# Two decode layers in one core: a ring of three places instead of four, one more key part kept on the chip, and the end of the second up matrix loaded in another shape

## The chip, the cores and the metric

The kernel runs on one core of a Trainium2 chip. The metric is device time in microseconds (us) for one execution of the whole program; each kernel is timed in several runs on the same chip, and the median is given. A profile of one execution of the program gives the detail: its busy times per engine (PE does matrix products, DVE, ACT and POOL elementwise work, SP only issues loads), its waits, and what the sixteen DMA engines moved.

## What is computed

Two layers, with the same weights and caches in both, each made of an attention block and a gated MLP, for one new token of a batch of two:

```python
def _A_ref(x, k_cache, v_cache, wq, wo):
    # B=2, Sq=1, D=576, H=32, Dh=128, Sk=8192
    q = (x @ wq).reshape(B, Sq, H, Dh).transpose(0, 2, 1, 3)
    scores = jnp.einsum("bhqd,bhkd->bhqk", q, k_cache) * (Dh ** -0.5)
    p = softmax(scores)
    o = jnp.einsum("bhqk,bhkd->bhqd", p, v_cache)
    return o.transpose(0, 2, 1, 3).reshape(B, Sq, H * Dh) @ wo

def _B_ref(x, w_gate, w_up, w_down):   # Df = 4608
    return (gelu(x @ w_gate) * (x @ w_up)) @ w_down

x = x + _A_ref(layernorm(x), k_cache, v_cache, wq, wo)
x = x + _B_ref(layernorm(x), w_gate, w_up, w_down)
x = x + _A_ref(layernorm(x), k_cache, v_cache, wq, wo)
x = x + _B_ref(layernorm(x), w_gate, w_up, w_down)
```

All of it is in float32. The two caches hold 268 MB each, and each layer reads both.

## The kernel before

**Items and parts.** The caches are cut into items: 30 items of two heads of one batch entry each (`PAIRS`), and four of a single head (`SINGLE`). An item's keys or values come in parts of 128 partitions by 16 rows of 128 numbers, `PART` = 2048 floats per partition, 1024 KB. A pair item has 8 parts, a single one has 4. The first layer walks through the items from first to last, the second from last to first, so that what the first layer read last can stay on the chip. The keys of the last two single items (62 and 63 in the names below) and the values of the last three stay whole. Of the item `SINGLE[1]`, which is third in the second layer, one key part of four stays: the first layer copies part 3 into a PSUM tile, `kept` (line 636), and the second copies it back into the place of part 0 (line 679).

**The arena.** All that is loaded goes into one tile, `space`, of `END` floats per partition. An `Arena` keeps track of what is live. Six slots of four parts each begin at 0; pairs of slots hold pair items. Between the layers the last slot's room, from `RING` on, is used as a ring of `NPLACE` places of `PLACE` = 2304 floats (9216 bytes per partition, 1152 KB for a whole place). In the second layer's MLP no ring is used: `fit` looks for the first free stretch in all of `space`.

**The queue of loads.** `plan_first`, `plan_mlp` and `plan_second` append every load, in order, to one list. `pump` issues loads from the head of the list for as long as there is room, and stops at the first one that has none; each time a reader is done with a piece (`done`), `pump` goes on. All loads are issued by SP, in this order. When the program runs, an issue waits until the last reader of the bytes it overwrites has finished, and everything behind it waits too. There are eight landing semaphores, taken in turn, so an issue also waits for the landing of the load eight before it.

**What goes through the ring.** In order: the eight pieces of `wo` in the first layer (`out_rows`, line 296); 18 pieces of the first MLP's gate and up (`split_rows` and `split_middle`, lines 248 and 258), each read as two or four loads; nine of the down matrix (`down`, lines 271 and 275); nine pieces of wq for the second layer (`of_half` and `half_rows`, lines 238 and 227); then three key parts of `SINGLE[1]` and one of `SINGLE[0]` (`one`, line 165). Before that, two places hold the products of the kept keys (`products`): the keys must not be overwritten, so the products of items 62 and 63 go there.

**Attention.** For each item, DVE multiplies the key parts by the query (line 644), POOL adds the two halves of the 128 products (line 661) and DVE sums the rest (line 664); ACT takes the exponentials (line 721); PE multiplies the weights with the values (line 762). For the first items of the second layer some of the work is moved to POOL and ACT. At the end PE multiplies with `wo` (line 812).

**The MLP.** After a layer norm (`norm`), `xt` holds the transposed input in nine blocks of 32 columns, one for each of the nine rows that a partition holds of the matrix halves. In the second layer `all_products` multiplies gate and then up: each of the nine half rows `u` of a partition has eight sixteenths of `HG` = 288 columns, and each is one matrix product (line 967). The list `GU` says how many half rows one load carries: three and three and three for gate, three, three, one, one, one for up. Then `activate` makes `hT`, and the down products follow (line 1004). `idle_products` (line 526) are products whose result nobody reads.

## Time and profile before

| | |
|---|---|
| time, median of 3 runs | 2686.63 us (2686.57 to 2686.77) |
| the profiled execution | 2686.79 us, span 2685.0 us |
| read from HBM | 1153.18 MB, 429 GB/s over the span |
| busy: PE, DVE, POOL, ACT | 914.4, 1806.0, 1161.8, 163.7 us |
| mean granted PE clock | 0.642 |
| the chain that ended last, by share | DMA 28%, DVE 13%, POOL 3% |

In the views, L644 is line 644 of the kernel. A row of the timeline gives the start and the length in us, the engine, the line, the operation and the tiles, the number of instructions merged, and in brackets the idle time of the engine before it and what ended it. A row of the windows gives the stretch, its length, the busy time of PE, weight loads, DVE, ACT and POOL with the number of instructions, the granted PE clock, the DMA engines' mean busy share (it can read slightly over 1, since packets overlap a little) and GB/s. A row of waits gives who waited for whom, the sum, the count, and the longest. Matrix products in float32 appear as two passes each, so a count such as x16 stands for eight products.

### The profile page before, as it was taken

The page shows a single profiled execution, that of the slowest core. Times are in us where ns is not written, and L with a number is a line of the kernel's source. Part 1 is how long each engine was busy: PE and PEld are TensorE (multiplying, and loading weights), DVE is VectorE, ACT ScalarE, POOL GpSimd, SP SyncE. Part 2 cuts the span into 40 slices and gives each one's busy share as a digit, 9 for nine tenths or more (in the row PEclk, how much of TensorE's full clock was granted, in tenths as well). Part 3 has the DMA queues.
Part 4 walks back from the last instruction along what each step waited for, and adds up shares of the span by engine and source line. Part 5 has one row for each costly group of instructions (what it writes and reads, how often), then busy time and mean ns, then how long its engine had stood idle before and what let it go on. Part 6 is the DMA issues. An engine that isn't in the chain of part 4 may idle for free. (4 is left out here: it accounts for less than half of the span.)

```text
span 2685.0 us, 17174 instructions
## 1 busy us (share of the span) xinstructions
PE 914.4 (34%) x7150; PEld 305.4 (11%) x7150; DVE 1806.0 (67%) x874; ACT 163.7 (6%) x786; POOL 1161.8 (43%) x261
## 2 busy tenths in 40 slices
PE   1323332332233233334663333233223323332356
PEld 0100010010001000111221101001000100010022
DVE  4876687677667766867037877667766776776640
ACT  0000000000000000000026000000000000000000
POOL 2543454354445444544028455445444543454420
PEclk7656666665666566566986665666566656656678
DMA  9999999999999999999999999999999999999998
GB/s 422 436 436 426 437 432 434 433 434 432 433 431 435 436 428 433 436 428 425 414 418 434 431 431 436 431 434 434 437 428 434 434 435 431 431 434 435 433 421 375
DMA packets 33950, 1154.30 MB, mean 430 GB/s; under 512 B 4152, under 2 KB 4176, under 8 KB 5968
## 3 DMA queue, kind: packets, MB, share of 16 engines
q1 hardware_dynamic: 33832, 1153.19, 99.8%
q8 instruction: 56, 0.92, 0.1%
q14 instruction: 22, 0.18, 0.0%
q10 hardware_dynamic: 40, 0.01, 0.0%
HBM read 1153.18 MB, written 0.00 MB: 429 GB/s over the span
## 5 line engine op out<-in xcount | busy, mean ns | idle before, releaser
L661 POOL TENSOR_TENSOR space<-space 128x3072 f32<-128x3072 f32 (+3 forms) x221 | 1128.6, 5107 | 1263.3 <-DVE space L644 1202.5
L644 DVE TENSOR_TENSOR space<-space,bank 128x6144 f32<-128x6144 f32 (+3 forms) x223 | 1112.7, 4991 | 560.2 <-DMA space<-in_A_k_cache_dram 496.8
L762 PE MATMUL acc<-space,prz 128*8 128x512 f32 x4096 | 594.6, 744 | 199.4 <-DMA space<-in_A_v_cache_dram 195.5
L664 DVE TENSOR_REDUCE S<-space 128x48 f32<-128x3072 f32 (+3 forms) x223 | 569.3, 2553 | 89.9 <-POOL space L661 89.6
L592 PE MATMUL bank<-qsb,pick 4*64 4x128 f32 (+1 forms) x256 | 46.3, 436 | 863.1 <-DVE space L644 853.1
L762 PEld LDWEIGHTS acc<-space,prz 128*8 128x8 f32 x4096 | 119.1, 104 | 616.3 <-issue 410.6
L784 PE MATMUL bank<-of,osb 128*32 128x2 f32 x512 | 40.9, 202 | 324.4 <-DVE osb L777 324.4
L713 ACT ACTIVATE nbs<-bank 128x2 f32<-128x2 f32 (+1 forms) x68 | 11.6, 171 | 1848.2 <-PE bank L698 1801.8
L592 PEld LDWEIGHTS bank<-qsb,pick 4*64 4x64 f32 (+1 forms) x256 | 20.7, 202 | 882.5 <-DVE space L644 863.2
L517 POOL TENSOR_TENSOR rstd<-ve,mhalf 128x1 f32<-128x1 f32 x4 | 2.2, 550 | 168.8 <-DVE ve L515 168.8
L690 PE MATMUL bank<-ident,m 128*1 128x128 f32 x68 | 19.5, 286 | 160.7 <-DVE m L688 160.5
L784 PEld LDWEIGHTS bank<-of,osb 128*32 128x32 f32 x512 | 35.9, 154 | 331.7 <-DVE osb L777 330.5
L978 DVE STREAM_TRANSPOSE o<-o 128x288 f32<-128x288 f32 x4 | 2.8, 691 | 94.5 <-ACT o L976 94.5
L729 PE MATMUL bank<-sums,unit 128*128 128x2 f32 x120 | 35.2, 363 | 87.0 <-ACT prz L721 87.0
L776 DVE TENSOR_TENSOR acc<-acc,diag 128x512 f32<-128x512 f32 x64 | 43.5, 680 | 22.0 <-PE acc L762 22.0
L721 ACT ACTIVATE prz<-S,nbs 64x128 f32<-64x128 f32 (+1 forms) x128 | 50.7, 396 | 17.3 <-POOL prz L711 14.4
L803 ACT ACTIVATE oT<-bank,rinv 32x8 f32<-32x8 f32 x110 | 28.5, 259 | 381.5 <-PE bank L784 380.8
L654 ACT ACTIVATE space<-space 128x128 f32<-128x128 f32 x164 | 48.3, 296 | 23.6 <-DVE space L644 21.7
L698 PE MATMUL bank<-m,unit 1*128 1x2 f32 (+1 forms) x136 | 39.0, 354 | 25.3 <-DVE m L696 25.3
L777 DVE TENSOR_REDUCE osb<-acc 128x128 f32<-128x512 f32 x64 | 44.3, 691 | 2.2
L521 DVE TENSOR_TENSOR x<-bank,x 128x144 f32<-128x144 f32 x4 | 1.2, 308 | 64.1 <-PE bank L1004 40.4
L729 PEld LDWEIGHTS bank<-sums,unit 128*128 128x128 f32 x120 | 30.1, 311 | 92.2 <-ACT prz L721 92.2
(73 smaller groups left out, 427.6 us busy)
## 6 DMA issues: line engine op xcount, KB each, us to landing
space<-in_A_v_cache_dram SPq DMA_DIRECT2D x8, 4096.0 KB
space<-in_A_k_cache_dram SPq DMA_DIRECT2D x6, 4096.0 KB
space<-in_A_wo_dram SPq DMA_DIRECT2D x15, 1152.0 KB
space<-in_A_k_cache_dram SPq DMA_DIRECT2D x15, 1024.0 KB
space<-in_B_w_down_dram SPq DMA_DIRECT2D x9, 1152.0 KB
space<-in_B_w_gate_dram SPq DMA_DIRECT2D x3, 3456.0 KB
space<-in_A_v_cache_dram SPq DMA_DIRECT2D x10, 1024.0 KB
space<-in_A_wq_dram SPq DMA_DIRECT2D x3, 3072.0 KB
```

What stands on the lines that cost most here:

```text
L592: nc.tensor.matmul(qb[n][to, :], pick[32 * c:32 * c + 4, r:r + 1].to_broadcast([4, P // it.heads]), qsb[32 * c:32 * c + 4, (h % 4) * DH:(h ...
L644: nc.vector.tensor_tensor(out=u[:, :rows, :], in0=t[:, :rows, :], in1=qb[n].unsqueeze(1).to_broadcast([P, rows, DH]), op=ALU.mult)
L654: nc.scalar.activation(u[:, j, :], u[:, j, :], AF.Copy, accum_out=S[n][:, k * JC + j:k * JC + j + 1])
L661: nc.gpsimd.tensor_tensor(out=half, in0=half, in1=u[:, :r, DH // 2:], op=ALU.add)
L664: nc.vector.tensor_reduce(out=S[n][:, k * JC:k * JC + own_rows(n, k, m)], in_=prod.pop((n, k)), axis=AX.X, op=ALU.add)
L698: nc.tensor.matmul(mT[n][:, :heads], ones[0:1, :], m1[:, :heads], start=True, stop=True)
L721: nc.scalar.activation(pr[at, lo:].rearrange("p (g e) -> p g e", e=4)[:, 0:it.rows // 2:2, :], s[at, :it.rows].rearrange("p (g r) -> p g r ...
L729: nc.tensor.matmul(tot[n][:, :ITEMS[n].heads], ones, rs.pop(n), start=True, stop=True)
L762: nc.tensor.matmul(accumulator(n)[32 * c:32 * c + 8, :], pr[:, at:at + 8], t[g // 4][:, g % 4 * 4:g % 4 * 4 + 4, :].rearrange("p j d -> p ...
L776: nc.vector.tensor_tensor(out=q, in0=q, in1=diag.unsqueeze(2).to_broadcast([P, 4, DH]), op=ALU.mult)
L777: nc.vector.tensor_reduce(out=t, in_=q.rearrange("p r d -> p d r"), axis=AX.X, op=ALU.add)
L784: nc.tensor.matmul(po[lo:lo + 32, i, :], t[:, i::GH], of, start=True, stop=True)
```

## The change

The ring has three places instead of four. The room behind it, `STAY`, holds part 2 of the keys of `SINGLE[1]` from the first layer to the second; part 3 stays in PSUM as before. Both copies are made by ACT when the first part of that item is multiplied in the first layer. The second layer reads two parts of that item instead of three. `END` shrinks by 256 floats. The products of the kept keys go to places 1 and 2 instead of 2 and 3.

In the second MLP, the up matrix's half rows 6 to 8 are one load of 128 partitions without the last two sixteenths of half row 8 (`upper_rows`). These two sixteenths, `LOWER` = 2, are loaded for all 128 rows onto partitions 0 to 63 (`lower_rows`): those of rows 0 to 63 and, beside them, those of rows 64 to 127. They come in eight loads of 8 partitions each (every fourth partition of 32), four before and four after the last gate load. PE takes them last, in four products over 64 partitions, for which `norm` adds a transpose of the upper 64 partitions' last block to the lower ones. Two small tiles change their place or grow by 32 columns.

```diff
--- before.py
+++ after.py
@@ -32,15 +32,17 @@
 PAD = 6
 NT = 4
 NI = DF // (NT * P)
+LOWER = 2
 CW = D // 4
 
 PART = JC * DH
 SLOT = 4 * PART
 NSLOT = 6
 PLACE = DF // 2
-NPLACE = 4
+NPLACE = 3
 RING = 5 * SLOT
-END = RING + NPLACE * PLACE
+STAY = RING + NPLACE * PLACE
+END = STAY + PART
 HELD = 5
 
 
@@ -239,6 +241,32 @@
 
         weights(("wq", 1, h, k), width, None, transfers)
 
+    def upper_rows(key, w, us, first, lower):
+
+        n = len(us) * w.shape[1] // 2 - lower * HG
+        rows = w.rearrange("r (s w) -> (r s) w", s=2).rearrange("(p u) w -> p (u w)", p=P)
+        lo = us[0] * w.shape[1] // 2
+        weights(key, n, first, lambda t: nc.sync.dma_start(t, rows[:, lo:lo + n]))
+
+    def lower_rows(key, w, first, lower):
+
+        width = w.shape[1] // 2
+        rows = w.rearrange("r (s w) -> (r s) w", w=width).rearrange("(e p u) w -> p e u w", e=2, u=NU)
+        rows = rows[:, :, NU - 1, width - lower * HG:]
+        weights(key, 2 * lower * HG, first, lambda t: None)
+
+        def eighth(at):
+            def make():
+                nc.sync.dma_start(ready[key][at], rows[at])
+                return True
+
+            return lambda: queue.append(make)
+
+        return [eighth(slice(lo + j, lo + 32, 4)) for lo in range(0, HALF, 32) for j in range(4)]
+
     def split_rows(name, w, h, u):
 
         rows = w[:, DF // 2 * h:DF // 2 * (h + 1)].rearrange("(m r) w -> m r w", r=NU)
@@ -279,7 +307,7 @@
     def products():
 
         def make():
-            at = [RING + k * PLACE for k in (2, 3)]
+            at = [RING + k * PLACE for k in (1, 2)]
             if not all(arena.clear(a, PLACE) for a in at):
                 return False
             ready["products"] = [part(arena.take(("products", k), at[k], PART)) for k in range(2)]
@@ -302,7 +330,7 @@
 
     single = [range(u, u + 1) for u in range(NU)]
     three = [range(u, u + 3) for u in range(0, NU, 3)]
-    GU = [three, three[:-1] + single[-3:]]
+    GU = [three, three]
 
     DOWN = [
         [[(t, i) for i in range(lo, lo + 4)] for t in range(NT) for lo in (0, 4)] + [[(t, NI - 1) for t in range(NT)]],
@@ -369,7 +397,7 @@
         last = PAIRS - 1
         k63, v63, k62, v62 = ("k", 1, SINGLE[3]), ("v", 1, SINGLE[3]), ("k", 1, SINGLE[2]), ("v", 1, SINGLE[2])
 
-        for k in range(3):
+        for k in range(2):
             one(("k", 1, SINGLE[1]), kc, SINGLE[1], k, None)
         for k in range(4):
             one(("k", 1, SINGLE[0]), kc, SINGLE[0], k, (k63, k - 1) if k else None)
@@ -405,9 +433,17 @@
                 for u in range(4):
                     split_rows("u", wu, h, u)
         else:
-            for g, (name, w) in enumerate((("g", wg), ("u", wu))):
-                for us in GU[g]:
-                    half_rows((name, layer, us[0]), w, us, 0)
+            for i, us in enumerate(GU[0]):
+                if i == 2:
+                    short = lower_rows(("u", layer, NU), wu, 0, LOWER)
+                    for make in short[:4]:
+                        make()
+                half_rows(("g", layer, us[0]), wg, us, 0)
+            for make in short[4:]:
+                make()
+            for us in GU[1][:-1]:
+                half_rows(("u", layer, us[0]), wu, us, 0)
+            upper_rows(("u", layer, GU[1][-1][0]), wu, GU[1][-1], 0, LOWER)
         for rows in DOWN[layer]:
             down(layer, rows)
 
@@ -434,7 +470,7 @@
     diag = consts.tile([P, 4], F32, name="diag")
     of = consts.tile([P, B], F32, name="of")
     both = ident.rearrange("p (c v b r) -> p b r v c", c=4, v=4, b=B)[:, :, :, 0, :]
-    eight = consts.tile([P, B, 4], F32, name="eight")
+    eight = once.tile([P, B, 4], F32, name="eight", tag="part")
     nc.vector.reduce_sum(eight, both, axis=AX.X)
     nc.vector.tensor_add(diag, eight[:, 0, :], eight[:, 1, :])
     nc.vector.reduce_sum(of, eight, axis=AX.X)
@@ -459,7 +495,7 @@
 
 
 
-    xt = consts.tile([P, PAD + NU * 32], F32, name="xt")
+    xt = consts.tile([P, PAD + (NU + 1) * 32], F32, name="xt")
     nc.vector.memset(xt, 0.0)
 
 
@@ -483,7 +519,7 @@
         return smalls[0][0:p, 0:n]
 
 
-    def norm(split=False, then=None):
+    def norm(split=False, lower=False, then=None):
         stats = work.tile([P, 6], F32, name="stats")
         nc.vector.bn_stats(stats, x)
         apart = work.tile([P, 4, 6], F32, name="apart")
@@ -511,6 +547,8 @@
         nc.vector.transpose(xt[:, PAD:PAD + 32 * u].rearrange("p (u q) -> p u q", u=u), xs)
         if then is not None:
             then()
+        if lower:
+            nc.vector.transpose(xt[:HALF, PAD + 32 * NU:], xs[HALF:, NU - 1, :])
         ve = work.tile([P, 1], F32, name="ve")
         nc.vector.tensor_scalar_add(ve, mv[:, 1:2], EPS)
         rstd = work.tile([P, 1], F32, name="rstd")
@@ -632,8 +670,11 @@
             if k == 0:
                 S[n] = work.tile([P, SK * 2 // P], F32, name="S")
             u = t = keys(n, k, m)
-            if n == SINGLE[1] and k == 3 and layer == 0:
-                nc.scalar.copy(kept, t)
+            if n == SINGLE[1] and k == 0 and layer == 0:
+
+                ready["k", 1, n] = {2: part(arena.take((("k", 1, n), 2), STAY, PART))}
+                nc.scalar.copy(ready["k", 1, n][2], keys(n, 2, 1))
+                nc.scalar.copy(kept, keys(n, 3, 1))
             if layer == 0 and n in KEYS_HELD:
                 u = ready["products"][k % 2]
             every = m * JC
@@ -930,7 +971,7 @@
 
     def mlp(layer):
         split = layer == 0
-        rstd = norm(split)
+        rstd = norm(split, lower=not split)
         if split:
             idle_products(3)
         hT = once.tile([P, 2, NI, 2, 2, B], F32, name="hT", tag="xc")
@@ -958,17 +999,28 @@
 
         def all_products():
 
+            def product(g, u, sixteenth, x, w):
+                v, c = sixteenth // 4, sixteenth % 4
+                of_lower = g == 1 and sixteenth >= 8 - LOWER
+                nc.tensor.matmul(
+                    acc[32 * c:32 * c + 4 * B, v, :HG], x, w,
+                    start=(g == 0 and u == 0), stop=(g == 1 and u == NU - 1 + of_lower),
+                )
+
             for g, name in enumerate("gu"):
                 for us in GU[g]:
-                    w = ready.pop((name, layer, us[0])).rearrange("p (u v c w) -> p u v c w", v=2, c=4, w=HG)
-                    for u in us:
-                        for v in range(2):
-                            for c in range(4):
-                                nc.tensor.matmul(
-                                    acc[32 * c:32 * c + 4 * B, v, :HG], window(u, 4 * g), w[:, u - us[0], v, c, :],
-                                    start=(g == 0 and u == 0), stop=(g == 1 and u == NU - 1),
-                                )
+                    w = ready.pop((name, layer, us[0])).rearrange("p (s w) -> p s w", w=HG)
+                    for k in range(w.shape[1]):
+                        u = us[0] + k // 8
+                        product(g, u, k % 8, window(u, 4 * g), w[:, k, :])
                     done((name, layer, us[0]))
+            key = ("u", layer, NU)
+            w = ready.pop(key).rearrange("p (e s w) -> p e s w", e=2, w=HG)
+            for e in range(2):
+                for k in range(LOWER):
+                    u = NU - 1 + e
+                    product(1, u, 8 - LOWER + k, window(u, 4)[:HALF], w[:HALF, e, k, :])
+            done(key)
 
         def activate(v):
 
```

## The prediction

> **What bounds the kernel now.** I read the page first: busy shares, the DMA line, the queues.
>
> ```profile
> span 2685.0 us, 17174 instructions
> PE 914.4 (34%) x7150; PEld 305.4 (11%) x7150; DVE 1806.0 (67%) x874; ACT 163.7 (6%) x786; POOL 1161.8 (43%) x261
> DMA  9999999999999999999999999999999999999998
> q1 hardware_dynamic: 33832, 1153.19, 99.8%
> q8 instruction: 56, 0.92, 0.1%
> ```
>
> No engine is busy for more than 67% of the span, while the DMA line stands at nine tenths or more in every slice but the last, and the main queue's packets fill 99.8% of sixteen DMA engines' time. The kernel is bound by the bytes it reads. Two questions decide the change: how many bytes go, and whether the DMA engines stay fed with a shorter ring. So I read the stretches around the middle of the run, and the first microseconds for the delay from an issue to the first byte (columns: us, busy us of the five engines with counts, granted clock, DMA share, GB/s).
>
> ```profile
> 1384.00:1433.00 49.00, 21.25 (x117) 6.66 (x115) 35.96 (x37) 30.83 (x191) 32.61 (x26) 0.69 1.01 421
> 1260.00:1280.00 20.00, 13.17 (x207) 5.94 (x201) 3.18 (x7) 0.61 (x3) 0.00 (x0) 0.99 1.01 420
> 0.00:1.00 1.00, 0.00 (x0) 0.00 (x0) 0.17 (x3) 0.00 (x0) 0.41 (x5) 1.00 0.00 0
> 1.00:2.00 1.00, 0.00 (x0) 0.00 (x0) 0.62 (x7) 0.00 (x0) 0.29 (x1) 1.00 0.95 246
> ```
>
> ```profile
> 0.74 0.39 SPq L227 DMA_DIRECT2D space<-in_A_wq_dram  x1
> ```
>
> In the middle the share is 1.01 too: nothing starves there with four places. The very first load is issued at 0.74 us and all engines are at work between 1 and 2 us, so the first byte comes 0.3 to 1.3 us after the issue. I allow 1 to 2.5 us where more loads are being issued, an estimate from that row.
>
> **The part that stays.**
>
> ```profile
> space<-in_A_k_cache_dram SPq DMA_DIRECT2D x15, 1024.0 KB
> space<-in_A_wo_dram SPq DMA_DIRECT2D x15, 1152.0 KB
> ```
>
> One of the fifteen single key parts is no longer read in the second layer: 1024 KB, or 1.049 MB, at 421 GB/s is 2.5 us. It would be the whole gain, if every later load moved up by as much. The price of keeping it is one more copy on ACT in the first layer.
>
> ```profile
> L636 ACT COPY kept<-space x1: 1856/1856/1856, 1218.9 to 1218.9; 128x2048 f32<-128x2048 f32 x1
> 1200.00:1220.00 20.00, 5.95 (x39) 2.35 (x39) 9.63 (x9) 1.58 (x4) 5.20 (x4) 0.70 1.00 429
> ```
>
> 1.86 us each, two instead of one, on an engine with 1.58 us of work in 20. Both are now issued at part 0, so DVE's in-place products of parts 2 and 3, and the softmax of the item before on ACT, queue behind 3.7 us. DVE has about 10 us idle in that stretch with the DMA share at 1.00: cost nothing, and 1.9 us if that cover were gone.
>
> **The shorter ring.** A load into a place waits until that place's last reader has finished. With three places it waits for the reader three loads back, which in before let the next load but one go. So I take, for each load, the issue time that the following load has now, and ask how long the engines still have work then. SP's queue is in order: everything behind the waiting load waits too. Steady stretches have room: a place holds 1152 KB, 1.18 MB or 2.8 us at 420 GB/s, two full places are 5.6 us of work, and readers free a place 1 to 2 us after its landing. The tight spots are where a reader is late for another reason. Four of them, with issues of SP and matmuls of PE that waited for a landing:
>
> ```profile
> 1258.46 2.95 SPq L296 DMA_DIRECT2D space<-in_A_wo_dram  x2
> 1296.75 0.47 SPq L258 DMA_DIRECT2D space<-in_B_w_gate_dram  x1
> 1372.97 0.33 SPq L227 DMA_DIRECT2D space<-in_A_wq_dram  x1
> 1383.99 8.29 SPq L165 DMA_DIRECT2D space<-in_A_k_cache_dram  x5
> 1396.03 5.06 SPq L165 DMA_DIRECT2D space<-in_A_k_cache_dram  x3
> 1405.07 3.50 SPq L165 DMA_DIRECT2D space<-in_A_v_cache_dram  x4
> 1408.67 33.83 SPq L165 DMA_DIRECT2D space<-in_A_k_cache_dram  x9
> 1432.83 0.33 SPq L165 DMA_DIRECT2D space<-in_A_k_cache_dram  x1
> ```
>
> ```profile
> 1285.37 1.16 PE L812 MATMUL bank<-space,oT 128*4 128x144 f32 x32 [0.93 <-DMA space<-in_A_wo_dram]
> 1299.48 1.16 PE L951 MATMUL acc<-space,xt 128*8 128x288 f32 x16 [0.35 <-DMA space<-in_B_w_gate_dram]
> 1375.51 1.04 PE L549 MATMUL acc<-space,xt 128*4 128x512 f32 x8 [1.03 <-DMA space<-in_A_wq_dram]
> 1390.38 1.04 PE L549 MATMUL acc<-space,xt 128*4 128x512 f32 x8 [1.04 <-DMA space<-in_A_wq_dram]
> ```
>
> First, the two places of the products are now two of three, so the second output weight, and the two value parts behind it, wait until 1258.46 (DVE's sum over the third key part), when only the third weight waited before. The sixth output weight lands at 1285.4; from the second to the sixth lie five weights and four value parts, 10.1 MB or 24.0 us, so the first weight lands near 1261.4 and 2.9 us of work are left at 1258.46. Second, at 1296.75 the first gate piece is read (the layer norm delayed it); that release now serves the fourth gate piece, whose forerunner lands at 1299.4: 2.7 us. Third, at 1372.97, again after a norm, the first quarter of wq is read; that serves the fourth quarter, and the third lands at 1375.4: 2.5 us. Fourth, the last of wq lands at 1390.3, and 19 parts of 1.049 MB are issued from 1383.99 until 1432.83 (five, three, four, and seven of the nine): 19.9 MB, 47.3 us, so they land at 1437.6. The load at 1432.83 waits for DVE, whose times hang on wq and not on the removed part. The engines have 4.8 us of work then, and 2.3 us once the part is gone.
>
> So 2.9, 2.7, 2.5 and 2.3 us of work stand against 1 to 2.5 us until the first byte. The last engine to finish does not starve, but what the others may run ahead shrinks to 0 to 1.9 us. That lead is used now: an instruction block (0.92 MB over 56, 16.4 KB) holds one engine, 0.62 us at a sixteenth of 421 GB/s, and a load has landed only when its slowest engine is through. Where the lead is gone, such a block holds up all sixteen. The bounds: nothing (leads stay) to four blocks, 2.5 us, and more if the first byte takes over 2.5 us (a rival below); a gain is excluded, since a release never comes earlier with fewer places. I take two blocks, 1.2 us: the two late spots have the least left.
>
> **The ninth half rows.** What stood in three loads of 1152 KB becomes one load of 128 partitions and eight of 8 partitions, with the same bytes. The eight issues cost SP some 0.33 us each (the wq row's length), 2.6 us, while a later load of this matrix is already waiting far ahead:
>
> ```profile
> 2603.68 49.37 DMA space<-in_B_w_up_dram
> 2659.82 0.18 DVE L988 TENSOR_SCALAR hT<-ga 128x36 f32<-128x36 f32 x1
> PE bank L1004 <- DMA space<-in_B_w_down_dram: 7.0, 6, 3.4
> 2647.54 6.73 PE L967 MATMUL acc<-space,xt 128*8 128x288 f32 x80 [2.31 <-DMA space<-in_B_w_up_dram]
> 2655.88 1.16 PE L967 MATMUL acc<-space,xt 128*8 128x288 f32 x16 [1.62 <-DMA space<-in_B_w_up_dram]
> ```
>
> Issue and landing lie 49 us apart: SP's 2.6 us are hidden. PE now has 26 products, 52 passes, after the last up byte instead of 16 passes: at 6.73 us for 80 that is 4.4 us against 1.16, so hT is 3.2 us later. Behind it PE waits 7.0 us in all for down weights; of the longest wait, 3.4 us until 2662.14, hT for the first half was ready near 2660, so about 1.3 us do not count and 5.7 remain. That hides 3.2 us; without it they would be the price. The added DVE transpose of one block of 64 partitions lies before gate weights that PE waits for: nothing.
>
> The halves of the sixteen engines are another matter. Their share in the last stretch:
>
> ```profile
> 2673.00:2674.00 1.00, 0.94 (x8) 0.18 (x3) 0.00 (x0) 0.00 (x0) 0.00 (x0) 1.00 0.95 380
> 2675.00:2676.00 1.00, 1.00 (x33) 0.81 (x26) 0.00 (x0) 0.00 (x0) 0.00 (x0) 1.00 0.66 274
> 2677.00:2678.00 1.00, 0.87 (x24) 0.49 (x24) 0.00 (x0) 0.00 (x0) 0.00 (x0) 1.00 0.46 189
> 2679.00:2680.00 1.00, 0.92 (x24) 0.54 (x24) 0.00 (x0) 0.00 (x0) 0.00 (x0) 1.00 0.43 173
> 2680.00:2681.00 1.00, 0.55 (x16) 0.33 (x16) 0.00 (x0) 0.00 (x0) 0.00 (x0) 1.00 0.07 25
> ```
>
> About half of the engines are done some 4 us before the others. The two sixteenths are 128 rows of 2304 bytes, 0.295 MB. If rows on upper partitions go through other engines than rows on lower ones, 0.147 MB leave one half and load the other: 0.147 MB at half of 421 GB/s is 0.7 us off the one and on the other. The end moves by -0.7 us if the late half is the one relieved, by +0.7 us if it is the one loaded; the rows don't say which. I take 0 and keep both ends. [...]
>
> **The sum.** -2.5 (part) + 1.2 (ring) + 0 (tail) = -1.3 us. The profiled execution took 2686.79 us (2685.0 of span), so 2685.5; the median of the runs, 2686.63, lies 0.16 lower, which makes the forecast 2685.3 us.
>
> **The rivals.** *All is kept, and the late half is relieved:* first bytes come within 1.3 us as at the start, leads stay, -2.5 - 0.7 = -3.2 us, 2683.4. For it speaks the 0.74 row, against it that all four spots fall near norms, with several loads being issued. *Slower than before:* first bytes take 3.5 us. Then the slowest engine starves too, by 0.6, 0.8, 1.0 and 1.2 us: 3.6 us, +1.1 and 2687.7; with the late half loaded 2688.4. It decides from 3.2 us on, where four shortfalls make 2.5. *The lower half is the late one:* the late engines get 0.7 us more at the end: -2.5 + 1.2 + 0.7 = -0.6 us, 2686.0. [...] *The whole middle starves:* a first byte over 4 us after its issue leaves every one of some 35 loads through the ring short by 0.3 us, 10 us or more, 2694. The share of 1.01 with 4.8 us in hand speaks against it.
>
> **How the numbers follow.** Forecast 0.40 (own range 2684.6 to 2686.0), all kept 0.15, slower than before 0.22, the lower half late 0.17, whole middle 0.06. The range, 2683.8 to 2688.2, leaves out the far case and parts of the two ends. A measurement of this kernel is told from no change at about 0.2%, 5.4 us. No case gains that much: 0.01 faster. Only the whole middle starving loses it: 0.07 slower; 0.92 within.
>
> **What would show it.** The main queue at 1152.13 MB; a DMA share a little under 1.01 after 1258, 1297, 1373 and 1433; PE's last wait for an up weight followed by 52 passes without a wait, and down products that wait less; in the last 8 us shares nearer to each other, or a longer stretch near 0.4. Wrong would be: a share of 0.9 over the middle, a down product that never waits, or a time over 2688.2.

## The result and the profile after

| | before | after |
|---|---|---|
| time, median | 2686.61 us (2686.46 to 2687.08, 11 runs) | 2693.51 us (2690.95 to 2694.4, 11 runs) |
| ratio, after to before, with its 95% interval | | 1.0024, 1.0016 to 1.0033 |
| the profiled execution | 2686.79 us, span 2685.0 | 2694.3 us, span 2692.5 |

The change makes the kernel 6.9 us slower, where 1.3 us less was forecast. These are lines of the page after: span, busy times, GB/s in 40 slices of 67 us, the main queue, and the chain of waits by engine.

```profile
span 2692.5 us, 17185 instructions
PE 915.0 (34%) x7154; PEld 305.8 (11%) x7154; DVE 1806.4 (67%) x875; ACT 165.5 (6%) x787; POOL 1161.7 (43%) x261
GB/s 421 435 436 434 433 430 436 431 434 433 434 432 434 434 436 429 432 430 415 403 374 422 435 436 434 431 434 432 434 434 434 433 432 432 433 435 435 433 421 384
q1 hardware_dynamic: 33592, 1152.14, 99.6%
DMA 34%; PE 10%; DVE 1%; POOL 0%; issue 0%; ACT 0%; SPq 0%; POOLq 0%
```

One part less is read, as meant, and no engine works longer by more than ACT's 1.8 us for the second copy. What changed is the rate in three slices between 1210 and 1410 us. The stages of the ring show it, first before, then after (columns: us, busy us of PE, weight loads, DVE, ACT and POOL with counts, granted PE clock, DMA share, GB/s).

```profile
1240.00:1258.00 18.00, 5.89 (x29) 1.96 (x33) 17.67 (x14) 0.61 (x3) 11.95 (x7) 0.50 0.98 420
1258.00:1290.00 32.00, 22.71 (x337) 9.85 (x325) 5.34 (x11) 0.61 (x3) 1.95 (x2) 0.93 1.01 417
1290.00:1320.00 30.00, 19.07 (x217) 7.08 (x218) 3.98 (x16) 0.73 (x2) 0.55 (x1) 0.94 1.00 409
1320.00:1345.00 25.00, 15.21 (x152) 4.80 (x147) 0.80 (x3) 0.73 (x2) 0.00 (x0) 0.93 1.01 422
1345.00:1375.00 30.00, 21.55 (x346) 10.73 (x346) 3.98 (x16) 0.47 (x2) 0.55 (x1) 1.00 1.01 415
1375.00:1400.00 25.00, 11.02 (x72) 2.87 (x72) 11.38 (x9) 8.21 (x50) 7.73 (x6) 0.85 1.01 419
1400.00:1430.00 30.00, 14.80 (x80) 4.54 (x80) 22.70 (x24) 21.15 (x129) 22.93 (x18) 0.67 1.01 421
1430.00:1460.00 30.00, 15.29 (x86) 4.70 (x86) 26.89 (x30) 23.29 (x153) 26.00 (x21) 0.67 1.02 433
```

```profile
1240.00:1258.00 18.00, 5.88 (x29) 1.98 (x33) 17.67 (x14) 0.61 (x3) 11.97 (x7) 0.50 0.95 408
1258.00:1290.00 32.00, 20.50 (x337) 9.48 (x325) 5.35 (x11) 0.61 (x3) 1.96 (x2) 0.99 0.99 406
1290.00:1320.00 30.00, 20.62 (x202) 6.52 (x200) 2.44 (x10) 0.00 (x0) 0.55 (x1) 0.83 1.00 398
1320.00:1345.00 25.00, 12.97 (x148) 4.35 (x145) 1.88 (x7) 0.97 (x3) 0.00 (x0) 1.00 1.00 400
1345.00:1375.00 30.00, 21.84 (x340) 11.47 (x340) 1.91 (x8) 0.97 (x3) 0.00 (x0) 0.89 0.99 380
1375.00:1400.00 25.00, 13.92 (x96) 3.24 (x94) 5.94 (x11) 2.67 (x13) 3.05 (x3) 1.00 0.95 360
1400.00:1430.00 30.00, 10.01 (x54) 3.67 (x46) 24.65 (x24) 19.48 (x128) 21.63 (x17) 0.65 1.00 393
1430.00:1460.00 30.00, 18.91 (x108) 5.94 (x112) 23.88 (x29) 22.32 (x138) 23.41 (x19) 0.67 1.02 432
```

Every stage of the ring is slower by 3 to 14%, and nothing is lost behind 1430 us. Taking the missing rate times the length of each row (12 of 420 in 18 us are 0.5 us, 59 of 419 in 25 us are 3.5 us, and so on), the rows add up to 11.6 us. Less the 2.5 us of the part that is not read, this is 9 us, where the two profiled executions lie 7.5 us apart. The rates are rounded to whole GB/s, and over the 2,400 us outside these rows half a GB/s is worth more than that difference. Read the last two columns together: the share stands at 0.99 to 1.00 in five rows in which 11 to 35 GB/s are missing. The share alone would have shown little.

**The round of a place.** How a stage loses can be followed on one place of the ring. These are the issue of the fourth down load, the products that read it, and the issue of the load that takes its place, in the timelines: with four places, with three, and, from an experiment below, with two.

```profile
1343.91 0.33 SPq L271 DMA_DIRECT2D space<-in_B_w_down_dram  x1
1353.87 1.16 PE L1004 MATMUL bank<-space,hT 128*4 128x144 f32 x32 [0.79 <-DMA space<-in_B_w_down_dram]
1355.09 0.33 SPq L271 DMA_DIRECT2D space<-in_B_w_down_dram  x1
```

```profile
1348.99 0.33 SPq L299 DMA_DIRECT2D space<-in_B_w_down_dram  x1
1356.58 1.16 PE L1056 MATMUL bank<-space,hT 128*4 128x144 f32 x32 [0.76 <-DMA space<-in_B_w_down_dram]
1357.80 0.33 SPq L299 DMA_DIRECT2D space<-in_B_w_down_dram  x1
```

With two places it is the second down load, since the products of the fourth took 1.91 us (at 1381.00) instead of 1.16:

```profile
1368.63 0.33 SPq L302 DMA_DIRECT2D space<-in_B_w_down_dram  x1
1374.11 1.16 PE L1040 MATMUL bank<-space,hT 128*4 128x144 f32 x32 [1.05 <-DMA space<-in_B_w_down_dram]
1375.33 0.33 SPq L302 DMA_DIRECT2D space<-in_B_w_down_dram  x1
```

A round takes 11.18 us with four places, 8.81 with three, 6.70 with two. Divided by the places, a load of 1.18 MB is taken up every 2.80, 2.94 and 3.35 us: 422, 402 and 352 GB/s. With two places hardly anything is queued ahead, so 6.7 us is near the least that a round takes, for a load whose transfer alone is 2.8 us. At 421 GB/s three places hold 8.4 us of transfer and four hold 11.2. So three places have 1.7 us to spare and four have 4.5, and the measured round with three is already past 8.4.

The trace also keeps marks on the landing semaphores: sixteen for each of these loads, taken here as one for each DMA engine, the last of them being the landing. They divide the three rounds:

| places | issue to the middle of the marks | middle to the last mark | last mark to the next issue |
|---|---|---|---|
| four | 7.8 us | 2.1 us | 1.3 us |
| three | 5.8 us | 1.8 us | 1.3 us |
| two | 4.9 us | 0.5 us | 1.3 us |

So in these rounds 0.8 of the 2.1 us between 6.7 and 8.8 are the queue ahead, 1.3 are the late engines, and the reader takes the same time. From the first to the last mark of a load lie 3.4 us on average before, 1.8 after and 1.2 with two places (the loads that landed between 1260 and 1395 us): the fewer the places, the less the engines can run ahead of the slowest.

**What follows an issue on a dry queue.** With two places, a load of up is issued at 1326.44, when nearly everything queued has been moved (the timeline, then the windows):

```profile
1326.44 0.47 SPq L279 DMA_DIRECT2D space<-in_B_w_up_dram  x1
```

```profile
1326.00:1328.50 2.50, 1.72 (x16) 0.41 (x15) 0.00 (x0) 0.00 (x0) 0.00 (x0) 0.61 0.46 85
1328.50:1331.00 2.50, 1.06 (x14) 0.27 (x6) 0.00 (x0) 0.00 (x0) 0.00 (x0) 1.00 0.95 394
```

From about 1328.5 on, 2.1 us after the issue, 394 GB/s move again. In the trace the packets of this load begin 1.3 us after the issue, at 1327.71, and each engine's first one takes 0.5 to 1.3 us, where most of those behind take 0.35. Theory A's "at least 2 us to the first byte" was the author's estimate.

**The worst spot after** is the fourth quarter of wq, behind the norm: its issue and the product that reads the third quarter in the timeline, then the windows around.

```profile
1379.40 0.47 SPq L240 DMA_DIRECT2D space<-in_A_wq_dram  x1
1381.73 1.04 PE L587 MATMUL acc<-space,xt 128*4 128x512 f32 x8 [0.97 <-DMA space<-in_A_wq_dram]
```

```profile
1379.00:1379.50 0.50, 0.50 (x8) 0.14 (x8) 0.00 (x0) 0.00 (x0) 0.00 (x0) 1.00 0.44 180
1379.50:1380.50 1.00, 1.00 (x10) 0.17 (x2) 0.00 (x0) 0.00 (x0) 0.00 (x0) 1.00 0.06 25
1380.50:1381.50 1.00, 0.27 (x2) 0.00 (x0) 0.00 (x0) 0.00 (x0) 0.00 (x0) 1.00 0.89 164
1381.50:1382.50 1.00, 0.77 (x8) 0.22 (x9) 0.00 (x0) 0.00 (x0) 0.00 (x0) 1.00 0.88 336
```

At the issue little is left in the queue: 25 GB/s between 1379.5 and 1380.5. And yet the third quarter is only read at 1381.73, when it has landed. Of the sixteen marks of its second load fifteen come between 1379.44 and 1380.06, the last at 1381.60: one engine is 1.5 us behind all the others. Four packets of 0.31 us run back to back from 1380.07 to 1381.30, so what is late is that engine's work and not the signal. Why it is late, no row shows.

### The profile page after: what moved, and what is told of

The parts are those of the page before. It is cut to its first block, busy times and chain, and to the rows that moved or that the text cites. A ratio compares the mean times of both kernels' runs of the same rounds, so it can differ in the third digit from the quotient of the medians.

```text
span 2692.5 us, 17185 instructions
## 1 busy us (share of the span) xinstructions
PE 915.0 (34%) x7154; PEld 305.8 (11%) x7154; DVE 1806.4 (67%) x875; ACT 165.5 (6%) x787; POOL 1161.7 (43%) x261
## 3 DMA queue, kind: packets, MB, share of 16 engines
q1 hardware_dynamic: 33592, 1152.14, 99.6%
## 5 line engine op out<-in xcount | busy, mean ns | idle before, releaser
L754 ACT ACTIVATE nbs<-bank 128x2 f32<-128x2 f32 (+1 forms) x68 | 11.6, 171 | 1820.1 <-PE bank L739 1773.7
L630 PEld LDWEIGHTS bank<-qsb,pick 4*64 4x64 f32 (+1 forms) x256 | 20.7, 202 | 881.0 <-DVE space L685 861.7
```

Of the source, the lines that this page charges most:

```text
L630: nc.tensor.matmul(qb[n][to, :], pick[32 * c:32 * c + 4, r:r + 1].to_broadcast([4, P // it.heads]), qsb[32 * c:32 * c + 4, (h % 4) * DH:(h ...
```

## The experiments

Theory A was that the ring costs everywhere, because the round of a place fits three places too closely; theory B, the prediction's, that it costs in four spots and the rest comes from elsewhere. Each time below is a median beside the kernel before on the same chip, with the ratio's 95% interval.

**The second up's loads alone.** Ring of four, no second part kept:

```
-NPLACE = 3
-STAY = RING + NPLACE * PLACE
-END = STAY + PART
+NPLACE = 4
+END = RING + NPLACE * PLACE
...
-        for k in range(2):
+        for k in range(3):
             one(("k", 1, SINGLE[1]), kc, SINGLE[1], k, None)
...
```

> The new second up load and its eight small loads alone, on the ring of four places, with three key parts of the item read in the second layer as in the kernel before. Theory A (the loss is in the ring: the round of one place, from issue over first byte, transfer, slowest engine and reader to the next issue, takes about as long as three places need to be moved): the tail is worth at most 0.7 us either way, 2685.9 to 2687.3. Theory B (the ring costs only the four tight spots of the prediction, 1 to 4 us, and the rest of the +6.9 us comes from the new loads of the up matrix): 2690 to 2693.

2686.86 against 2686.65 us, ratio 1.0000 (0.9992 to 1.0009). The new loads are no part of the loss.

**The ring alone.** The kernel before with three places:

```
-NPLACE = 4
-END = RING + NPLACE * PLACE
+NPLACE = 3
+STAY = RING + NPLACE * PLACE
+END = STAY + PART
...
+            if where == STAY:
+                at = arena.take((key, k), STAY, PART)
...
-            one(("k", 1, SINGLE[1]), kc, SINGLE[1], k, None)
+            one(("k", 1, SINGLE[1]), kc, SINGLE[1], k, None if k < 2 else STAY)
```

> The kernel before with a ring of three places, nothing else: the same 1153.2 MB are read, up as before; the third key part of the item is loaded into the room behind the ring. Theory A: the ring alone costs what the changed kernel lost between 1250 and 1420 us, 9 to 10 us, so about 2696. Theory B: 1 to 4 us, 2688 to 2690.5.

2697.61 us, ratio 1.0036 (1.0023 to 1.0048): 11.0 us for the shorter ring, 6 to 13 by the interval, since these five runs scatter (2693.63 to 2698.93).

**The change without the second up's loads.** `GU` and `all_products` as before:

```
-    GU = [three, three]
+    GU = [three, three[:-1] + single[-3:]]
...
```

> The changed kernel with the up matrix of the second layer loaded and multiplied as before (three, three, one, one, one half rows), ring of three and the kept part as changed. Theory A: the changed kernel's time within 1 us, 2692.5 to 2694.5. Theory B: the loss goes, 2685 to 2688.

2695.38 us, ratio 1.0030 (1.0019 to 1.0040), 8.7 us, 0.9 above theory A's range and far above B's. Between the ring alone, 11.0, and this lie 2.3 us, which fits the 2.5 forecast for the part that is no longer read; with the scatter of both runs that closeness may be luck. The parts, 11.0 for the ring, -2.3 for the part and 0.2 for the loads, add up to 8.9, where the change costs 6.9. The 2 us between are within the intervals and have no shown cause.

**Two places.** On the kernel just shown:

```
-NPLACE = 3
+NPLACE = 2
-STAY = RING + NPLACE * PLACE
+STAY = RING + (NPLACE + 1) * PLACE
...
-            at = [RING + k * PLACE for k in (1, 2)]
+            at = [RING + k * PLACE for k in (0, 1)]
...
```

> As e3_without_lower, but the ring has two places (the first part of the item read after it goes to the room that the third place had). Theory A: the round of a place without a queue ahead is at least 2 us to the first byte, 2.8 us of transfer, 0.5 to 1 us of slower engines and 1.2 to 1.6 us of reading, 6.5 to 7.5 us for two places of 2.8 us: each of some 35 loads through the ring costs 0.45 to 0.95 us more than its transfer, and the second and later output weights start late: 15 to 40 us over e3, 2708 to 2733. Theory B: the same few spots, a place of 2.8 us less in each of four: at most 11 us over e3.

2728.78 us, ratio 1.0155 (1.0141 to 1.0169): 33.4 us over the one before. Four, three and two places form a row, 0, 11 and 44 us for the ring (the last with the 2.3 us of the part added to its 42.1), which four spots can't make.

**Where in the ring.** Three places until the last down load and four from wq on, and the other way round:

```
+        if key[0] not in ("wo", "g", "u", "gu", "d"):
+            at = self.take(key, (STAY, RING + 2 * PLACE, RING, RING + PLACE)[self.late % 4], n)
...
```

```
+        if key[0] not in ("wo", "g", "u", "gu", "d"):
+            at = self.take(key, RING + self.late % 3 * PLACE, n)
...
```

> Ring of three for the output weights, gate, up and down, as in e2_ring3_only, but four places again from the first quarter of wq on (the room behind the ring, in which e2 put one key part, is the fourth). Same bytes as the kernel before. e2 was 11 us slower. Theory L (three places have too little to spare everywhere, so all loads share in the loss): 4 to 7 us over the kernel before, 2690.5 to 2693.5. Theory N (the loss is made by the norm ahead of wq and the short places there, since a quarter of wq fills only 1024 KB of a place): 0 to 3 us, 2686.6 to 2689.5.

> The other half: the kernel before with four places until the last down load, and three for the nine pieces of wq and the key parts behind them (the third key part of the item goes to the fourth place, as it went behind the ring in e2). Theory L: 10 of some 45 loads and one of two norms: 3 to 6 us, 2689.5 to 2692.5. Theory N: 8 to 11 us, 2694.5 to 2697.5. Under either the two prices add up to the 11 us of e2 within 3 us; if they don't, the loss needs both stages, a late start carried on.

2692.01 us, ratio 1.0018 (1.0009 to 1.0027), and 2690.57 us, ratio 1.0014 (1.0006 to 1.0023): 5.3 and 3.8 us, 9.1 together where the whole ring cost 11.0. Both are within theory L's ranges and outside theory N's. Both stages lose, and within the intervals the two prices add. The second has about a quarter of the ring's loads and two fifths of the loss. The windows of the first, then of the second:

```profile
1290.00:1320.00 30.00, 18.65 (x210) 6.33 (x201) 2.67 (x11) 0.50 (x1) 0.56 (x1) 0.94 1.01 402
1320.00:1345.00 25.00, 13.94 (x144) 4.49 (x144) 1.62 (x7) 0.47 (x2) 0.00 (x0) 0.93 0.99 387
1375.00:1400.00 25.00, 15.57 (x94) 3.33 (x94) 7.97 (x10) 3.84 (x21) 4.17 (x4) 0.88 1.01 418
```

```profile
1290.00:1320.00 30.00, 18.73 (x213) 6.83 (x216) 3.71 (x14) 0.60 (x2) 0.56 (x1) 0.94 1.00 409
1320.00:1345.00 25.00, 15.40 (x160) 4.97 (x152) 0.58 (x3) 0.85 (x3) 0.00 (x0) 0.93 1.01 421
1375.00:1400.00 25.00, 12.88 (x70) 2.64 (x70) 9.10 (x6) 6.62 (x40) 6.40 (x5) 0.79 0.99 396
```

The rate follows the number of places: 387 with three places and 421 with four between 1320 and 1345, 418 with four and 396 with three behind 1375. A late start carried on can't be it, for the first kernel is back at 418 as soon as it has four places.

**Slower reads, on three places and on four.** Without idle products the granted clock was 0.60 to 0.73 in the four stages from 1290 to 1400 us on three places (0.83 to 1.00 in the changed kernel) and 0.66 to 0.72 on four (0.85 to 1.00 before), and PE's reads lasted longer:

```
     def idle_products(n):
+        return
...
```

> The changed kernel without any idle products. Theory F: one block less, and PE's clock lower: 0 to 1 us less than the changed kernel from the block, some more from slower reads. Theory G: the reads last longer at the lower clock (2.0 us instead of 1.2 us for a piece at a clock of 0.5) and each release comes 0.8 us later: with 35 loads 10 to 25 us more, 2703 to 2718.

> The kernel before without any idle products: the same slower reads as in e11_no_idle, on the ring of four. Theory L (the round of a place, from its issue to the release by its reader, has about 1.5 us to spare in three places and 4.3 us in four, and any delay beyond that, by a norm, a low PE clock or a late engine, stops all sixteen engines): the fourth place takes up the slower reads, 0 to 2 us over the kernel before, 2686.6 to 2688.6. Theory M (a lower clock costs in other ways, after the ring's stage or at the end): as much as on the ring of three, 6 to 8 us, 2692.5 to 2695.

2700.99 us on three places, ratio 1.0052 (1.0039 to 1.0065), and 2688.79 on four, ratio 1.0006 (0.9997 to 1.0015), 0.2 above theory L's range and well under M's. The groups of PE from 1258 to 1410 us, of after, then of the two (a group's busy time, mean, and what ended the idle time before):

```profile
L992 PE MATMUL acc<-space,xt 128*8 128x288 f32 x288 | 24.0, 450 | 19.5 <-DMA space<-in_B_w_up_dram 10.4 <-DMA space<-in_B_w_gate_dram 8.4 <-ACT o L1028 0.7
L587 PE MATMUL acc<-space,xt 128*4 128x512 f32 x72 | 9.4, 592 | 9.4 <-DMA space<-in_A_wq_dram 8.6 <-ACT qs L684 0.6 <-DVE ve L553 0.2
```

```profile
L988 PE MATMUL acc<-space,xt 128*8 128x288 f32 x288 | 31.9, 576 | 22.7 <-DMA space<-in_B_w_up_dram 12.5 <-DMA space<-in_B_w_gate_dram 7.7 <-DVE ve L553 1.8
L583 PE MATMUL acc<-space,xt 128*4 128x512 f32 x72 | 14.9, 938 | 10.2 <-DMA space<-in_A_wq_dram 8.2 <-DVE ve L553 2.0
```

```profile
L947 PE MATMUL acc<-space,xt 128*8 128x288 f32 x288 | 31.2, 579 | 18.4 <-DMA space<-in_B_w_up_dram 10.9 <-DMA space<-in_B_w_gate_dram 5.7 <-DVE ve L515 1.8
L545 PE MATMUL acc<-space,xt 128*4 128x512 f32 x72 | 13.5, 859 | 8.0 <-DMA space<-in_A_wq_dram 5.5 <-DVE ve L515 2.0 <-ACT qs L639 0.5
```

Gate and up take 31.9 and 31.2 us instead of 24.0, so the reads are slowed alike. On three places that costs some 7 us over the changed kernel, on four 2.0 over the kernel before (not told from 0 by its interval): the fourth place takes up what the reader does late. The amount for three places was under the 10 us or more that had been expected.

**Finer loads.** If the round is too long, loads of half the columns should shorten it. Three kernels split more and more of them, the down loads like this:

```
-                nc.sync.dma_start(t.rearrange("p (i c) -> p i c", c=D), src[:, 0])
+                to = t.rearrange("p (i c) -> p i c", c=D)
+                for lo, hi in ((0, 2), (2, 4)) if layer == 0 else ((0, len(rows)),):
+                    nc.sync.dma_start(to[:, lo:hi], src[:, 0, lo:hi])
```

> The changed kernel, with each first-layer load of the output and the down matrix that goes through the ring (but the last of each) issued as two loads of half the columns. A half's issue then waits only for the products that read that half, and the first products only for the first half's landing. Theory A, the round: it is shorter by half a transfer (1.4 us) and half a read (0.5 us), about as much as was missing; the down loads' part of the loss (about 3 us of 9 to 10) and some of the output weights' 0.7 us go: 2689.5 to 2691. Theory C (three places leave fewer bytes queued, and the engines move them more slowly, whenever the places are freed): within 1 us of the changed kernel, 2692.5 to 2694.5, or slower by the shorter rows.

> As e5, and the eight quarters of wq in the ring issued as four loads each (even and odd partitions, two column halves) instead of two. Theory A: most of the 3.6 us lost there goes too: 2686 to 2688. Against it, still theory A but with another wait: an issue waits for the landing of the load eight before it, which is then two places back instead of four, so the third place cannot be filled before the one two back has landed: no gain over e5, or 1 to 3 us slower than e5. Theory C: as e5.

> As e6, and the 16 split pieces of gate and up as four loads each too. Theory A without the landing wait: the last 1.6 us goes, 2684.5 to 2686.5, below the kernel before. Theory A with the landing wait of eight loads: gate and up, which are 18 of the 35 loads, lose more than now: 2692 to 2700. SP's issues at 0.5 us each, four for 2.8 us of transfer, would not bind.

2695.23, 2696.33 and 2696.13 us, ratios 1.0032 (1.0020 to 1.0045), 1.0036 (1.0024 to 1.0049), 1.0038 (1.0024 to 1.0051): no gain. Theory A's forecast for the first, 2689.5 to 2691, failed, and theory C's, the same or slower, was met. The last one's windows show where the gain went.

```profile
1345.00:1375.00 30.00, 21.82 (x348) 9.98 (x341) 4.48 (x16) 0.97 (x3) 0.55 (x1) 1.00 1.03 408
1375.00:1400.00 25.00, 17.21 (x84) 3.55 (x78) 3.37 (x2) 2.68 (x13) 2.50 (x2) 0.80 0.92 317
```

Down gains, 408 instead of 380 GB/s, and wq loses more, 317 instead of 360. That four loads per place run into the landing of the load eight before was expected for wq. SP's wq issues between 1374 and 1402 us do wait 3.0 us for landings of wq, 0.9 in the changed kernel; but gate and up, also with four loads per place, move 408 and 410 GB/s instead of 398 and 400 between 1290 and 1345, so this was not shown apart. With the output and down loads alone split, down moves 405 instead of 380, and gate and up, whose loads are as they were, 388 and 393 instead of 398 and 400. Why the whole gained nothing stays open, and theory C is not excluded by these runs.

**The value parts first.** Two value parts go ahead of the second output weight:

```
-        for g in groups(0)[:2]:
-            out_rows(0, g)
+        out_rows(0, groups(0)[0])
...
-                for g in groups(0)[2:4]:
+                for g in groups(0)[1:4]:
```

> The changed kernel with the second output weight behind the first two value parts of the last item in the queue instead of before them, so that these 2.1 MB (5 us) are issued at about 1234 us and not after the products' place is free at 1258 us. Theory A: the hole between 1250 and 1260 us (0.83 of the DMA engines' time, 337 GB/s) closes, 0.5 to 1.7 us less than the changed kernel, 2692 to 2693; the rest of the loss, in gate, up, down and wq, stays. Theory D (the whole stage is late because it begins late, and follows from this hole): most of the loss goes, 2685 to 2688.

2693.55 us, ratio 1.0027 (1.0017 to 1.0036): between 1240 and 1260 us it moves 420 GB/s (390 in the changed kernel), so the first hole closes, and the time stays. The 0.5 to 1.7 us that theory A expected are less than these ten runs scatter by (2689.83 to 2696.68); theory D, by which most of the loss would go, is excluded.

**Instruction blocks.** The prediction had priced the ring by them, with an estimate of 0.62 us a block; in the trace before the 56 packets of that queue took 1.07 us in the median. Each idle product of 256 columns became eight of 32, on the changed kernel and on the kernel before:

```
-        for _ in range(n):
+        width = 2 * P // parts
+        for _ in range(parts * n):
...
```

> The changed kernel, with each of the 52 idle products between 1258 and 1410 us (256 columns) replaced by eight of 32 columns, so that PE spends about as long on them but fetches some 1,450 more instructions, five to six more blocks of 16 KB (the instruction queue carried 0.92 MB in 56 blocks for about 14,300 PE instructions). Theory F (the ring of three has no slack, so each block that holds one DMA engine for 1.0 us holds up the landing, the reader and then all sixteen engines; the nine blocks of this stage are the 9 to 10 us lost): 5 to 6 us more than the changed kernel, 2698 to 2700. Theory G (the loss comes from PE reading late and slowly, and the blocks are only a sixteenth of their length each): within 1 us of the changed kernel if PE's reads keep their length.

> The kernel before with the same tiny idle products. Theory F: with a fourth place of slack a block costs its bytes only and its engine catches up: 0.3 to 1 us more than the kernel before, 2687 to 2687.6. Theory G: the same, 2687; if it is slower by 4 us or more, blocks cost their length whatever the ring, and the loss of the ring of three is something else.

2696.24 us, ratio 1.0031 (1.0019 to 1.0043), and 2689.21 us, ratio 1.0008 (0.9999 to 1.0017). Both profiles have 62 blocks instead of 56. The six cost about 2.4 us on three places (9.3 over before, where the change costs 6.9) and 2.2 on four, some 0.4 us a block. The intervals are too wide for a price, and neither theory's ranges were met. But the 5 to 6 us that theory F needs on the short ring did not come, and the four places lost about as much: blocks alone don't make three places slow.

**Shorter reads.**

```
+            n = EQ if start or layer == 0 else EQ // 2
...
+                    n = HG if key == steps[0][0] and k == 0 else HG // 2
```

> The changed kernel with half of the columns of each gate and up product of the first layer and of each wq product of the second left out (but in the first product of each sum), all loads as they are, so that PE has read a place about 0.5 us earlier in 26 of the 35 loads. Theory L: without idle products the reads were 19 us longer in sum and the time grew by 7.5 us; 13 to 14 us less should give back 2 to 5 us of the loss, 2688.5 to 2691.5. Theory M (the reads' length plays no part; what starves the engines is only the time from issue to the first byte and the norms): within 1.5 us of the changed kernel, 2692 to 2695.

2693.62 us, ratio 1.0024 (1.0015 to 1.0033), as the changed kernel. But the means to shorten the reads did little: with fewer columns the granted clock was 0.50 between 1320 and 1345 us (1.00 in the changed kernel), and gate and up still took 20.7 us instead of 24.0, wq 8.4 instead of 9.4: 4.3 us less, where 13 to 14 had been meant. The time is in theory M's range, but the run decides nothing.

## Why the prediction was wrong

**The ring is the step that failed.** It was priced at 1.2 us, bounds 0 to 2.5, and costs 11.0 when made alone (6 to 13). Two sentences carried that price.

*"Steady stretches have room: ... two full places are 5.6 us of work, and readers free a place 1 to 2 us after its landing."* A round does fit, by 1.7 us, but the room is used up: the measured one takes 8.81 us of 8.4. The stretch from the output weights to down, three quarters of the ring's loads, costs 5.3 us, more than half of it away from the named spots: 35 of 422 GB/s in the 25 us from 1320 are 2.1 us, 16 of 415 in the 30 us behind them 1.2 (399 there in that run). The prediction knew that a load lands with its slowest engine (at 1381.60 the last mark, at 1381.73 the read), but used it at the four spots only. In the steady stretches it set the 5.6 us against the reader alone. Counted for the middle engine of the round with three places, they shrink by the 1.8 us that it is done before the landing and by 1.3 of reading until the next issue: 2.5 us are left (an estimate from that one round), and new data take 2.1. That leaves no room for a reader or an engine that is late, and what one is late by goes round the ring to all the others.

*The work left at the issue.* At the fourth quarter of wq 2.5 us were said to be left, counted to the third quarter's landing. In the changed kernel next to nothing was, and the third quarter still landed 2.2 us after that issue. The prediction saw that the leads of the other engines would shrink, to 0 to 1.9 us, and then priced that by two blocks of instructions. The leads were the buffer itself, as the marks and the rows at 1379 us show: when fifteen engines are dry, their time is gone, whatever the last one does.

**The first byte was right.** 1 to 2.5 us were allowed; on a dry queue the packets began 1.3 us after the issue, and the rate was back after 2.1. So the rival "slower than before", with its 3.5 us, names the wrong cause. The rival *"the whole middle starves"* had the place, the kind of loss (a little on each of some 35 loads) and the time, 2694 against 2693.51, with a chance of 0.06. Its condition, a first byte over 4 us after the issue, isn't needed.

**What spoke against it was misread.** The share of 1.01 was taken as proof that nothing starves. The rows after have 0.99 to 1.00 with 380 to 406 GB/s: the share counts a packet's time, however long it takes for its bytes. In the trace the packets of 9216 bytes between 1345 and 1375 us took 375 ns on average after and 352 before. The clearest row is at 1380.5, behind the issue at 1379.40: a share of 0.89 with 164 GB/s, with first packets of up to 1.15 us where the usual one takes 0.31. So the share of 0.9 over the middle, named as a sign of being wrong, never came, while the time over 2688.2 did. In the changed kernel a share of 1.00 went with 433 GB/s from 1200 to 1220 us and with 398 from 1290 to 1320.

**Right were** the bytes (1152.14 MB in the main queue) and, as far as the scatter lets it be seen, the 2.5 us for the part (2.3 between two experiments). So were the copies on ACT, hidden: 1200 to 1220 us still move 433 GB/s. The end, 0 and at most 0.7 either way, is not contradicted: 0.2 us measured (0.9992 to 1.0009, too wide to tell 0 from 0.7). The last wait for up is followed by 52 passes, and the waits for down weights that were to hide them fell from 7.0 to 2.2 us (timeline, then waits):

```profile
2663.84 6.36 PE L1005 MATMUL acc<-space,xt 128*8 128x288 f32 x52 [4.43 <-DMA space<-in_B_w_up_dram]
```

```profile
PE bank L1056 <- DMA space<-in_B_w_down_dram: 2.2, 3, 1.1
```

The passes took 6.4 us where 4.4 were counted. The eight loads of 8 partitions, on which two rivals hung, leave eight marks each in the trace instead of sixteen, so they seem to run on eight engines; which eight, no row shows, and none shows rows on upper and on lower partitions going through different engines, on which the 0.7 us either way rest. Their issues took SP 0.68 us each (median), where 0.33 were counted.

**Still open** is why single engines fall behind, which is 1.3 of the 2.1 us between the least round (6.7) and the measured one (8.8), and why finer loads did not help. The division by marks is of one round of each kernel only.

## What to carry to other kernels

The depth of a ring is a latency, not only room: take one place's round, from its issue over first byte, transfer, slowest engine and reader to the next issue, and give the ring as many places as keep the memory busy that long, with the longest delay of a reader (a norm, a low clock) on top. Here four places with 4.5 us to spare absorbed slower reads (2.0 us lost) and three with 1.7 did not (some 7), so a buffer that saves an estimated 2.5 us of reading cost 11 (6 to 13) by taking a place. Judge a starved queue by GB/s in each stage against the same stage before, and count the work left for the average engine, not to the landing.

## What the runs showed of the hardware

- In the changed kernel the DMA share stood at 0.99 to 1.00 in the stages from 1258 to 1375 us at 380 to 406 GB/s; before, it stood at 1.00 to 1.01 there, at 409 to 422.
- With two places and next to nothing queued, the rate was back at 394 GB/s 2.1 us after the issue at 1326.44. The load of 1.18 MB issued at 1368.63 was read 5.5 us later, though at 421 GB/s it is 2.8 us of transfer.
- The first and the last of a load's sixteen marks lay 3.4 us apart on average with four places, 1.8 with three and 1.2 with two; at 1379 us one engine was 1.5 us behind the other fifteen.
- Six more instruction blocks of 16 KB went with 2.2 to 2.4 us more on either ring, which the intervals do not tell from nothing.
- On three places without idle products the granted clock was 0.60 to 0.73 in the stages from 1290 to 1400 us (0.83 to 1.00 with them), and gate and up lasted 31.9 us instead of 24.0.
- Kernels with three places scatter: 2690.95 to 2694.4 us here and 2690.96 to 2699.85 without the second up's loads. The kernel before ran from 2686.46 to 2687.08 beside the first and from 2686.35 to 2689.04 beside the second.
